# Attention by buckets, top-2 experts and a channel mix on one core: three new tables of order, engines and buffers

## The chip, the cores and the metric

The kernel runs on one core of one Trainium2 chip. The metric is the device time of one execution in microseconds (us). Before the change the median of three runs is 452.78 us (450.99 to 452.79).

## What is computed

The inputs are q, k and v of two batches, eight heads, 768 positions and 64 elements, float32. The reference has three stages, each on the result of the one before.

```python
# 1: attention inside hash buckets
q_bucket, k_bucket = buckets of the signs of q @ proj, k @ proj     # six bits each
scores = scale * q @ k.T,  -1e9 where the buckets differ
x = softmax(scores) @ v                       # heads side by side: 2 x 768 x 512
# 2: two of four experts of causal attention
w = softmax of the two largest of x @ w_gate
out = sum over e: w_e * (causal softmax(x wq_e (x wk_e).T) @ (x wv_e) @ wo_e)
# 3: channel mix, with x_prev the row before
xk = mu_k * x + (1 - mu_k) * x_prev;  xr likewise with mu_r
result = sigmoid(xr @ w_r) * (relu(xk @ w_k) ** 2 @ w_v)
```

## The kernel before

The 1536 rows of the two batches are cut into twelve row tiles of 128 (tile i belongs to batch i // 6). Each tile goes through all three stages: eight score products `s_i_h` of bucket attention, one per head, each followed by a softmax and the product with v (`x_i_g`, four heads each); the expert stage (`qk`, `vg`, scores `se`, `y`, output `o`); and the mix (`h` for the hidden layer, `r` for the gate, `v` for the way down). float32 products are made from float16 parts: an operand is split into a high part (a copy to float16) and a low part (the rest), and three products are added.

- **Softmax.** DVE takes the scores out of PSUM (`P<-s`, `P_m<-se`, with the row's extreme as its accumulated output), ACT makes the exponent in place. For twelve (tile, head) pairs, all eight heads of tile 0 and four of tile 1 (`F32T`), PE then transposes the float32 result (`tp`). For the 84 others ACT or POOL makes the high part `PHL`, POOL the low part, a transposing DMA on SP's queue turns it to `PT`, and PE multiplies `PT` with v. A product of PE on a `PT` that has not landed would wait for that DMA.
- **Mix.** DVE makes `o`, then four `m32k` and four `m32r`; `mk` and `mr` are their float16 parts. ACT makes `t` and `k2h` of the hidden layer, DVE `h` and `k2l`, and ACT the gate `e` with the sigmoid. Exp and sigmoid are functions of different tables on ACT, and the build puts an `ACT_TABLE_LOAD` wherever the next function is not in the table that is loaded.
- **Buffers.** PSUM has two slots of tag `s` for scores and four of tag `d` for everything else; SBUF has 13 large slots `b3` (P, PHL, PT, k, v), 40 `b2`, 4 `x2t` and 2 `b4`.

The program is first recorded: class `Program` takes down 2540 operations (`add`), each with its engine and the operations it must follow. Then `arrange` (line 205) applies three tables, and `issue` (line 220, whose call is L225) emits the operations in the order that the table gives. So L225 is the line of every row, and rows are told apart by engine and tile.

```python
for o, e in zip(self.ops, unpack(engines, np.uint8)):
    if e:
        o.move("PVAG"[e])
self.order = [self.ops[i] for i in unpack(table, np.uint16)]
...
for t, h in zip(tiles, unpack(homes, np.uint8)):
    if t.slot:
        t.kw.update(tag=f"{t.slot[1]}_{h}", bufs=1)
```

`ENGINES` moves a copy or a high part to DVE (V), ACT (A) or POOL (G); `Op.move` rewrites the call. `ORDER` is a permutation of the 2540 operations, and thereby the order on each engine and each queue. `HOMES` gives each tile its slot within its tag: two tiles of one slot are in it one after the other, so the later one's first writer waits for the earlier one's last reader.

Of the kernel before, what the change touches and what calls it, by code (L numbers as in the profile page):

```python
# [1001 lines left out]
C^lGHrz4@iR`LNR$l=VkgLssc-?b$1yM#HbD>g$XT!m=El2_1F~XjEQ)FH2`+>}xCkP{Jt&NMF%Q1R>9iQ~;ZdDR?O`x9!zGZLtKu7+2IJs9^n|pS4x8drOpi0@EoQ(W
kP{w2RC);0VH!oFzi<~c$FjH^_CRFX3y<J2MAL7$pM;{*K6r*F^l#h`f8d{37yrTUcmUqvbL<7<AqKt27MO=)(lPpg|Kfl61U}+Re1X^CIK`q9^b~$z2Yd!fCn-C;!jA
Y8K8F|Z5_-cax(>@RHXWe6e2@-NC(O?U_!Z>i9ki3;5YSir1vk<S_!$$@LHL3R=q7BUU38ds(@-eL@u?6O=FM~qZbK0+%JXS8Eugq`2iDLY+Cqsa3MHm^bO^T6LRv&Ks
T&sK5}XT?P<K2Gi)k&Lrge0LN^(*{oJC!*IIpK(cm$HsQd&kwAvw*aPn?4KU|&22U2!k<$8B^RdSFCYLM{0+rJ<D68++mmSWc~YIL@JgI35`X;b)#pgK-F^q6;(tS5Rj
dg@hAu626AC)S6e)2;4v;aVGS`bmXuNSL300k-qRxT%9LkTb_)m=_`-M^mJT3UZS5l19gF4SnyXqsZ($t<)Q986@O#JF*uKY=WpDDYj90|3s<No=cl}MmB!*3dIPoiJ8
!2V^bW33J}OSD=qR0~qVy;C;=i~N7oc<WE4+vE)SC-Z2`WY(AR}F;#$16vLKf=4fAC6Ik*DDe8is{v9NwgunvI%pR+@>~sU*$9+8j&U@!y<-N>NkJM9sJ(cjC@miGPDG
JOl62Et-yXcsAaqRjw=Cp$Al$N>ewOgPCbA=A^zh4_CXoyw?50^YJ{aaSJdP<)(X7ikowJT8QghX)Z%$sWO+N3RICE(tWB#OK}PI;S11}%kW}cgcl*Qt4vks5-h_(T!p
LB3am!y+(5nzQQRsl%T*a&IUd4S;3}kdzXQ3|SdYKKBdX7Xc_<&#1a25N;PO12W4eDigJbs{{(%2Dq5BioU{tpfYf^QpMK$OLH)M6uTy0WL<kn()&L-VBmNT~=H{fFmu
D*9}BW}VL{4>>|by$~@JHx)582j-NjP9P&GwRRJX#gj7v0Z&i;f~@HYDy#cFplK66vMqB@0!yneo3$B5WXgGqj?OEWpOE8GipHfs0oeZBrXX?a1H4l9mC_;g5J{!jOgO  # L1010
HllXxqa#Ebc<9P>8<~J1AZO3hx3@7k3ZbUP9CMU-!{Do5BbYAaL;#S<?GP=z;i&yeTisa(pMwi7Ub(!2$4)_br=1p$1OXjw?Ioz1m^D0i|B4B10-)(g}F(U55v@W&F>a
w})?h|cuyK%dVgsXWTf2BPb&+T)+Qd??8kueI!#os8WOXJ#5JnT-bsU0=&``r?bkDn>GJLM8!dz#O^D2Mx<deCXtftK<Cw}IF2U$6xeVo%EDI?@@}k{0k0x0W~ZPn5@X
qR!NX{)W6R5$1FETz+@Z^`@ilALvVcXou@c-{@aB=03rH(2okZg6;==r$6a0I_tX8CXTIt&|X}~QL&*1{F`>VeYhW&@c}IA{-K{BhA!fN=^*|`pWz3cbDJ4B8vYDlppg
# [86 lines left out]
```

## Time and profile before

| what | value |
|---|---|
| median of three runs | 452.78 us (450.99, 452.78, 452.79) |
| profiled execution, device time | 453.12 us |
| its span, first to last instruction | 451.3 us |
| PE busy | 430.6 us, 95% of the span |
| DVE busy | 348.4 us, 77% |
| ACT busy | 311.6 us, 69% |
| POOL busy | 347.3 us, 77% |
| PE's granted clock over the span | 1.000 |

The profile is of one execution, whose device time is 1.8 us over its span and 0.34 us over the median of the runs. A busy PE is one with a matmul in its pipeline, so its busy time is an upper bound on its work. DMA share above 1.00 in a row means that the packets of several queues overlap.

### The profile page before, as it was taken

The page shows a single profiled execution, that of the slowest core. Times are in us where ns is not written, and L with a number is a line of the kernel's source. Part 1 is how long each engine was busy: PE and PEld are TensorE (multiplying, and loading weights), DVE is VectorE, ACT ScalarE, POOL GpSimd, SP SyncE. Part 2 cuts the span into 40 slices and gives each one's busy share as a digit, 9 for nine tenths or more (in the row PEclk, how much of TensorE's full clock was granted, in tenths as well). Part 3 has the DMA queues.
Part 4 walks back from the last instruction along what each step waited for, and adds up shares of the span by engine and source line. Part 5 has one row for each costly group of instructions (what it writes and reads, how often), then busy time and mean ns, then how long its engine had stood idle before and what let it go on. Part 6 is the DMA issues. An engine that isn't in the chain of part 4 may idle for free.

```text
span 451.3 us, 14823 instructions
## 1 busy us (share of the span) xinstructions
PE 430.6 (95%) x6009; PEld 335.3 (74%) x6009; DVE 348.4 (77%) x906; ACT 311.6 (69%) x502; POOL 347.3 (77%) x375
## 2 busy tenths in 40 slices
PE   3899999989999999998999999999999999999997
PEld 2777878767888765884798668889666766976675
DVE  3799999999999998899798878766866666474432
ACT  5899979878878766787857787785456853265121
POOL 5997999998999969899999768997767856337130
...
GB/s 275 225 233 216 219 189 182 207 162 190 185 226 190 211 184 192 120 240 179 154 176 205 140 158 179 124 184 166 179 109 116 171 137 81 108 13 179 70 23 49
DMA packets 219701, 73.86 MB, mean 164 GB/s; under 512 B 211048, under 2 KB 215408, under 8 KB 219632
## 3 DMA queue, kind: packets, MB, share of 16 engines
...
## 4 chain that ended last, share of the span: by engine, by line
PE 43%; ACT 4%; DVE 4%; DMA 3%; issue 3%; POOL 3%; POOLq 0%; DVEq 0%; ACTq 0%
PE h L225 10%; PE v L225 9%; PE x L225 5%; PE s L225 4%; PE r L225 4%; DMA PT<-PHL 2%; PE qk L225 2%; PE se L225 2%; POOL PHL L225 2%; PE o L225 2%; PE vg L225 2%; PE y L225 2%; ACT P L225 2%; ACT L225 1%; DMA yT<-hl_y 1%
## 5 line engine op out<-in xcount | busy, mean ns | idle before, releaser
L225 POOL TENSOR_TENSOR PHL<-P,PHL 128x768 f16<-128x768 f32 x84 | 142.4, 1701 | 15.6 <-ACT PHL L225 13.6
L225 ACT ACTIVATE P<-P,mx 128x768 f32<-128x768 f32 x96 | 87.8, 931 | 16.2 <-DVE P L225 14.1
L225 DVE TENSOR_SCALAR_CACHE_REDUCE P<-s 128x768 f32<-128x768 f32 x96 | 90.3, 949 | 7.8 <-PE s L225 5.7
L225 PE MATMUL s<-y,x 128*128 128x384 f16 x384 | 77.5, 328 | 3.2 <-DVE P L225 3.1
L225 PE MATMUL h<-mk,WK 128*128 128x128 f16 x1152 | 74.4, 219 | 0.0
L225 PEld LDWEIGHTS <-WK 128*128 128x128 f16 x1152 | 67.7, 98 | 4.3
L225 PE MATMUL v<-WV,k2h 128*128 128x512 f16 (+1 forms) x208 | 57.8, 363 | 0.9 <-DVE y L225 0.9
L225 PEld LDWEIGHTS <-PT 128*128 128x128 f16 x1512 | 52.6, 98 | 6.2 <-issue 1.7
L225 PE MATMUL x<-vh,PT 128*128 128x65 f16 x1008 | 56.4, 194 | 0.6 <-DMA PT<-PHL 0.3
L225 PEld LDWEIGHTS <-x 128*128 128x128 f16 x480 | 38.5, 98 | 21.2 <-issue 3.5
L225 POOL TENSOR_SCALAR PHL<-P 128x768 f16<-128x768 f32 x42 | 36.7, 875 | 7.0 <-ACT P L225 5.1
L225 PE MATMUL x<-vl,PT 128*128 128x64 f16 x504 | 41.4, 193 | 0.0
L225 POOL TENSOR_TENSOR PHL_m<-P_m,PHL_m 128x512 f16<-128x512 f32 (+2 forms) x24 | 33.4, 1401 | 7.2 <-ACT PHL_m L225 6.6
L225 PE MATMUL v<-WV,k2l 128*128 128x512 f16 (+1 forms) x104 | 37.7, 363 | 0.0
L225 PE MATMUL qk<-xT,WQK 128*128 128x128 f16 x576 | 37.1, 219 | 0.0
L225 ACT ACTIVATE PHL<-P 128x768 f16<-128x768 f32 x42 | 34.9, 835 | 2.4 <-POOL PHL L225 1.5
L225 ACT ACTIVATE t<-h 128x512 f32<-128x512 f32 x24 | 14.2, 590 | 32.4 <-PE h L225 32.4
L225 PE MATMUL r<-WR,mr 128*128 128x512 f16 x144 | 35.7, 379 | 0.1
L225 PEld LDWEIGHTS <-WQK 128*128 128x128 f16 x576 | 33.7, 98 | 1.2
L225 PEld LDWEIGHTS <-k2h 128*128 128x128 f16 x208 | 18.8, 98 | 15.9 <-issue 1.5
L225 DVE SCALAR_TENSOR_TENSOR h<-h,t 128x512 f32<-128x512 f32 x24 | 16.6, 693 | 13.7 <-ACT t L225 13.5
L225 ACT ACTIVATE P_m<-P_m,bias_m 128x512 f32<-128x512 f32 (+2 forms) x24 | 19.3, 818 | 8.8 <-DVE P_m L225 8.7
(175 smaller groups left out, 928.1 us busy)
## 6 DMA issues: line engine op xcount, KB each, us to landing
...
PT<-PHL SPq DMA_TRANSPOSE x84, 4.2
```

The lines of the kernel that those rows point to most:

```text
L225: getattr(getattr(self.nc, engine), method)(*[real(a) for a in args], **{k: real(a) for k, a in kw.items()})
```

## The change

The three table strings are replaced; no other line of the kernel differs. The rows of the tables are compressed text, so the first line of each stands here for it.

```diff
 ORDER = """
-c-jTQ0{|FC3;@93Kgrj&ZQHhO+qP}nwr$(C&8;2Uxw}&kFaXF6ksuFLg}i`}56VDIr~z@I8kB_-P#p?Dfc#Jp>OeWD3-O>9)P{;s2u=Y(e24;-pfXf}!cYW~KvLKYePB
...
+c-jq@gAy3X5&(C!GaK8sZQHhO+qP}nwr$%s?~+4u&U@d`Ro&IzsWTTGJ8`*PXK)T&9v9ceb4y)bx6DOx`CNV%$yId)+;SJ+t#D;rRJYO<bP-%3*Vz?zMO-4c%2jhQTv?
...
 HOMES = """
-c-lo&*<#yB3?s<7hf1o{U2CP-a_b}i|A&ilnyeq}WJUx*0F=n*2Puj|OtOeZfkGp|3xfqg3_O;gJT~K@73mXrB;z3->G<0!qyzkqwXEXZFR`DnAFu-Z7y2&tD)L9{A9f
...
+c-l2oi+18V5Yx=~5kF|yaFgveEF>(H|Nq0QX-nWZ;Mf{TBM11tL}OOJN0<f`Q!@#iP!&ZO#6&C&FiXNg3aS_s{3E_!`2iOhZ-dA$SQZ44cah)F{{#^zzybOO{eb)d{)w
...
 ENGINES = """
-c-rk%%M!#O2$SUh|9Q95mlb4zvA3li>meW}KwEnlw*~#?Fx-Is#rKgX2x>F>b%$8X1!4P}VT>Sfat;S4eLVBCGOI)YSoP$e7(O41Zz5yDjK#taStb#vfKuQYJ<kkf<rR
...
+c-qaCQ38V?3`1$&{qMZFsVhRU;LrF#1R6>Rp_HnyRXYCk8&I)h0`;i22FDy~yicF%I5&s75?@r6bg^{jzm#5bY6)K}?B|h#WAK?;v%f`>cs^;D{oZ0Ns}9vM%Qm-lT$B
...
```

Both programs have the same 2540 operations. PE has the same matmuls (6009 in the trace of before). Some 175 operations run on another engine: of the high parts `PHL` 24 go from POOL to ACT and 19 from ACT to POOL; of the copies `y` out of PSUM seven go from ACT to DVE and four back; of the copies `x` seven from DVE to ACT and three back; and single ones of `vnh`, `x2t`, `kT`, `mr`, `mk` and others. DVE has 736 operations instead of 738, ACT 481 instead of 478, POOL 370 instead of 371. 972 of the 1279 tiles that have a slot get another one. ACT's table loads are 20 instead of 16.

The first piece is DVE's order at the beginning: `prhl` is the split of the hash projection, `nbq` and `nak` the low parts of the first query tile and of the keys. Before:

```order
L225 CAST prhl_75<-pr32_72 128x6
L225 SCALAR_TENSOR_TENSOR nbq_81<-q32_0_79,nbq_81 128x8x64
L225 SCALAR_TENSOR_TENSOR nak_0_1_1_102<-k32_0_1_1_84,nak_0_1_1_102 128x12x64
L225 TENSOR_TENSOR prhl_75<-pr32_72,prhl_75 128x6
L225 SCALAR_TENSOR_TENSOR nak_0_1_0_104<-k32_0_1_0_95,nak_0_1_0_104 128x12x64
```

And in the change:

```order
L225 CAST prhl_75<-pr32_72 128x6
L225 TENSOR_TENSOR prhl_75<-pr32_72,prhl_75 128x6
L225 SCALAR_TENSOR_TENSOR nbq_92<-q32_0_83,nbq_92 128x8x64
L225 COPY x2_0_109<-tr_x2_0_104 128x512
L225 SCALAR_TENSOR_TENSOR nak_0_0_1_96<-k32_0_0_1_94,nak_0_0_1_96 128x12x64
```

The second row of `prhl` now comes ahead of the first `nbq`, and one `nak` stands where three stood.

The second piece is DVE's order in the middle of the program. `P_6_h` takes the scores of head h of tile 6 out of PSUM, `P_m5` those of an expert of tile 5, `y_4`, `rse_4` and `y32_4` finish tile 4's experts, `vl` is a low part of v, and `qT_5`, `kT_0` are the low parts of tile 5's expert queries and keys. Before, these are rows 345 to 353 of DVE's order:

```order
L225 TENSOR_SCALAR y_4_4144<-y_4_4144,gs_4_3384 128x4
L225 RECIPROCAL y_4_4144<-y_4_4144 128x4
L225 TENSOR_TENSOR rse_4_4353<-y_4_4144,g_4_3383 128x4
L225 SCALAR_TENSOR_TENSOR vl_1_0_4202<-v32_1_0_1_4116,vh_1_0_3594 128x768
L225 TENSOR_TENSOR y32_4_4376<-y_4_4144,rse_4_4353 128x256
L225 SCALAR_TENSOR_TENSOR qT_5_4369<-qk_5_4187,qT_5_4369 128x256
L225 SCALAR_TENSOR_TENSOR nbq_81<-q32_7_615,nbq_81 128x8x64
L225 SCALAR_TENSOR_TENSOR kT_0_1248<-qk_5_4187,kT_0_1248 128x2x128
L225 TENSOR_SCALAR P_6_4_4389,mx_6_4008<-s_6_4_4342 128x768
```

In the change, rows 356 to 364, of which the last frees the PSUM slot that PE's `se_5_1_0` (second score product of tile 5's experts) is given by the new `HOMES`:

```order
L225 TENSOR_SCALAR y_4_4188<-y_4_4188,gs_4_3667 128x4
L225 RECIPROCAL y_4_4188<-y_4_4188 128x4
L225 TENSOR_TENSOR k2l_2_4152<-h_2_4_4170,k2h_2_4094 128x512
L225 TENSOR_TENSOR rse_4_4374<-y_4_4188,g_4_3666 128x4
L225 TENSOR_SCALAR P_6_6_4404,mx_6_3928<-s_6_6_4378 128x768
L225 TENSOR_TENSOR y32_4_4406<-y_4_4188,rse_4_4374 128x256
L225 TENSOR_TENSOR z_q7_4362<-z_q7_4362,zl_q7_4402 128x8x6
L225 TENSOR_SCALAR nbq_92<-z_q7_4362 128x8x6
L225 TENSOR_SCALAR P_6_4_4411,mx_6_3928<-s_6_4_4355 128x768
```

`h_2_4` and `k2l_2` of the mix and the evictions `P_6_5`, `P_6_6` now stand around the same `y_4` chain, and `kT_0` of tile 5 has gone further ahead.

The third piece is ACT's order around the first sigmoids: `e_0<-r_0` and `e_1<-r_1` are sigmoids, `P_5_h` in place the exponent of head h of tile 5, `WV2` and `wd_v2` the weight split. Before, directly after one `ACT_TABLE_LOAD`:

```order
L225 ACTIVATE e_1_3082<-r_1_2997 128x512
L225 ACTIVATE PHL_m3_1_3115<-P_m3_1_2861 128x512
L225 ACTIVATE wd_v20_0_3134<-raw_v20_0_3043 128x512
L225 ACTIVATE e_0_3141<-r_0_3096 128x512
L225 ACTIVATE yT_2_3152<-tr_y_2_3146 128x256
L225 ACTIVATE WV2_0_3169<-wd_v20_0_3134 128x512
L225 ACTIVATE wd_v25_0_3190<-raw_v25_0_3102 128x512
L225 ACTIVATE PHL_5_2_3226<-P_5_2_3025 128x768
L225 ACTIVATE x2t_2_2204<-o_2_3209 128x4x128
L225 ACTIVATE WV2_5_3260<-wd_v25_0_3190 128x512
L225 ACTIVATE vnh_0_524<-vg_4_3245 128x4x64
L225 ACT_TABLE_LOAD
```

In the change:

```order
L225 ACTIVATE WV2_5_3238<-wd_v25_0_3178 128x512
L225 ACT_TABLE_LOAD
L225 ACTIVATE e_0_3240<-r_0_3162 128x512
L225 ACTIVATE wd_v20_0_3306<-raw_v20_0_3153 128x512
L225 ACT_TABLE_LOAD
L225 ACTIVATE P_5_6_3244<-P_5_6_3244,mx_5_2902 128x768
L225 ACTIVATE WV2_0_3337<-wd_v20_0_3306 128x512
L225 ACT_TABLE_LOAD
L225 ACTIVATE e_1_3339<-r_1_3302 128x512
L225 ACT_TABLE_LOAD
L225 ACTIVATE P_5_4_3277<-P_5_4_3277,mx_5_2902 128x768
```

Two sigmoids that stood under one load now have a load each, with an exponent between them.

## Rows read from the trace of the kernel before

**Rows 1.** The page's part 1: PE's busy us, share of the span, instructions.

```profile
PE 430.6 (95%) x6009; PEld 335.3 (74%) x6009; DVE 348.4 (77%) x906; ACT 311.6 (69%) x502; POOL 347.3 (77%) x375
```

**Rows 2.** PE's waits: waiting row, releaser, us in total, times, longest us.

```profile
PE tr_x L225 <- DVE nbq L225: 6.6, 1, 6.6
PE s L225 <- DVE P L225: 3.1, 4, 1.0
...
PE tr_x L225 <- DVE kT L225: 0.6, 1, 0.6
...
PE x L225 <- DMA PT<-PHL: 0.3, 1, 0.3
```

**Rows 3.** The page's part 6: KB each is left out, us to landing.

```profile
PT<-PHL SPq DMA_TRANSPOSE x84, 4.2
```

**Rows 4.** Windows of the span, busy us of each engine (instructions), overlapping stretches.

```profile
core 0: us, PE busy (x) PEld busy (x) DVE busy (x) ACT busy (x) POOL busy (x), PEclk, DMA share, GB/s
0.00:30.00 30.00, 20.68 (x230) 16.73 (x230) 20.08 (x49) 22.12 (x39) 22.91 (x39) 1.00 0.91 255
...
60.00:90.00 30.00, 28.38 (x468) 23.75 (x466) 29.02 (x78) 25.78 (x47) 28.92 (x31) 1.00 1.08 202
...
0.00:122.00 122.00, 107.48 (x1376) 89.48 (x1377) 108.40 (x265) 103.24 (x188) 106.81 (x133) 1.00 0.95 210
0.00:152.20 152.20, 137.68 (x1857) 113.88 (x1858) 136.73 (x343) 128.14 (x232) 136.22 (x165) 1.00 0.98 210
0.00:211.83 211.83, 194.77 (x2683) 157.61 (x2684) 190.18 (x465) 173.10 (x296) 189.94 (x217) 1.00 0.99 201
211.83:451.34 239.51, 235.88 (x3326) 177.64 (x3325) 158.23 (x442) 138.51 (x207) 157.36 (x159) 1.00 0.75 130
```

**Rows 5.** Timelines of DVE and PE: start us, us, row [idle before <-releaser].

```profile
211.37 0.41 DVE L225 SCALAR_TENSOR_TENSOR kT<-qk,kT 128x256 f16<-128x256 f32 x1
...
211.83 0.38 PE L225 MATMUL tr_x<-ident,nbq 128*128 128x128 f16 x4 [0.60 <-DVE kT L225]
```

**Rows 6.** The chain of waits, 205 to 226: start us, us, what, count.

```profile
218.25 0.67 PE v L225 x3
218.92 1.30 PE se L225 x14
220.22 0.45 PE tr_x L225 x8
...
220.89 1.10 PE x L225 x36
```

**Rows 7.** DVE by form: busy us, mean ns of one, idle before it, releasers.

```profile
L225 DVE TENSOR_SCALAR_CACHE_REDUCE P<-s 128x768 f32<-128x768 f32 x96 | 90.3, 949 | 7.8 <-PE s L225 5.7 <-POOL PHL L225 0.8 <-PE x L225 0.6
...
L225 DVE SCALAR_TENSOR_TENSOR m32r<-o,mu,x2t 128x128 f32<-128x128 f32 x48 | 15.6, 342 | 0.2
...
L225 DVE DVE_READ_ACCUMULATOR P<-s 128x1 f32 x96 | 7.8, 82 | 0.0
...
L225 DVE SCALAR_TENSOR_TENSOR WK<-wd_k,WK 128x512 f16<-128x512 f32 x8 | 5.5, 682 | 0.0
...
L225 DVE SCALAR_TENSOR_TENSOR kT<-qk,kT 128x256 f16<-128x256 f32 x12 | 5.0, 416 | 0.2
...
L225 DVE COPY x<-tr_x 128x512 f16<-128x512 f16 x11 | 4.5, 415 | 0.2 <-ACT x L225 0.2
L225 DVE COPY y<-tr_y 128x768 f16<-128x768 f16 x8 | 4.4, 554 | 2.2 <-PE tr_y L225 2.2
```

**Rows 8.** ACT by form, the table loads.

```profile
L225 ACT ACT_TABLE_LOAD x16 | 20.5, 1283 | 3.9 <-issue 2.0 <-PE r L225 1.4 <-DVE P_m_p L225 0.2
```

**Rows 9.** Timeline of DVE at the start.

```profile
5.70 0.17 DVE L225 CAST prhl<-pr 128x6 f16<-128x6 f32 x1 [5.70 <-DMA pr<-in_proj_dram]
...
7.92 0.15 DVE L225 TENSOR_TENSOR prhl<-pr,prhl 128x6 f16<-128x6 f32 x1
```

More of the change, by code (lines that the diff above doesn't have):

```diff
@@ L1002 @@
[L1002 to L1013, printed above, removed]
@@ new lines @@
+46`&NPb5XG&RD{w{1J<~)F00Gt=DBfhryK9OyWuVut#zp&hbsfMAsWtil^~~^<QhXXZ3J~72Q-0oZZy_}o~{<Ogw(LWMaOX%17l(u7=!sCC#-i1-FV#K#^NH^7TUXv&>
+AYkQ7r(OV1mm9?Vt)Qb`fx+TjDmkHqg<vf?n>p7KGleJpiVMLXa6Ix{p*CcDc0B%d)@-R|GP^UH2>GhKRV^MZ%G;C?Ixnc_AJ2alb)U$On0Va0T~uv2X%@f~Jt&?QxOu
+o;#*{-9&5#lQ0`hcE7_uHwBx+Wc&<eAv@f658P{b1N&W7_z9l4srb+xaEyXe+*B7+pTIPH3U%QvJaUg+3pk<E@h|urW}wIVGRu91XYdPrgHi4n9(2cXntSGchCg6Geu3
+QdCp>lkKoool{oHqW?q0a(kjtIGjTjqW!6uA@C$R&(bl2P~_X0L!Z~GS#;eYS}w%`vqg$FRQ>j-)1BW%U~E&*P516(KAfv52uEXDV5!|lYln3wWVLcHl#<1XBdd+;FMa
@@ new lines @@
+`|Z)DjvcDblWY*_&D1Yq?wo)4`U%JOi6H#yW<>g!)|ciCB;K-79Mu<u{+Gh6}TK$ViB6|y1)@vluFQ17Y}E+u5iq)!M#|Fj=MQH7kj~4>;b)@4-}`K&>xava=d^?Z~+d
+7g_r^_;s{uWqu>)Q!q3zf)?+NKMkQ%9T*7{E85iS77!Q*GU=<F8K`;PP;{>QqUECF%4D)azq{1{f7&77%nCr&CRlJ5%Aw3R(p-_XyLI%u&DUl!>B4o!**pkxXPqYEQP)
+*8=>97^$!LO7Tvtn!dna*H7%z^olVHh06C0GOna$+qifWOeMR1~{YF1+BzL2;bv3gQeXgdTd(G$?`7L7^C4bdBgY+K!EBAAX}*(1vEhY&eT^peLQfOD;EdpxRUt=fXVr
+ok~$D>_zjT3ALs3cpWdhj#QeixCO8fuDYhwn_jy&?gkddoA}n%p-%Lj{-i&s8I_?j_!m{6cdj!nh0<6a+fg4{49#f?l*2`^3@Xxl*VT1%3Aiqm#TBp~KDdu=6Wqm>0Nj
@@ new lines @@
+O;%hDiP$@S<qmZPq;8dgCCyn`FzS2u(zVkP{W5<?}bOjT$g)u)6^Tp6q2KXeQKr3bhH?qOA`imP}qt%341l<HsudWh99Ij?2rweTMeBjLWLd>>cyZ!QI|;p%Ao2!GIUY
+Dnw&clXT&{_dXQAFd`w=0qHUYhewH!tLoX{^{01On#0pur|KLsBG{IV{uAO0^KMbdv+X=ThLKB1W)i4zQ(>(7Y{=NjKuw@KSkrDFn~r-G8jq8Aq5<PQIrzu<6EqUO>r`
+fr7?62HbZQV&g1Af#NiXr44Y#rPRvPo8a2U&n3_+*2b@7M_#GzW_521KVGEo>6Dd7!;L)^^H}iP<8RK(Wo=LN46F0^QG@B;TREh%`cnfdi>6C>7Y~_qRhq7`{i~zr2ck
+F@N`Bz*?UoaxX<xJc_vT-E%h>_tdzQ;72ls{oF{0*bPJc<jeXgzI#c)Sf(Q)cdsx%e-ao##_Si3fdfA8&`Pu!MHNXIx70Ap!Koez=Bmat_|X3uq_&j{A8R<mNn_m)Fuy
@@ new lines @@
+xQtriH*AX==oIgUgpdf@;6hqQ8|eTqr@!4I%Ex;kKWFp*xB|SBcX2`f16$)ke#+l*F8%9@@+SHd|HA*=Za&0CxG<mQLcD_h#(yv>9N~ZQKio`v_{abA+YZ~~8Ggn;&`}
+Bg<j(Rrj-k<@CGLfzyqNaEekjR6(V+t#;|_8Fig9ti$3z#nBgTO9yp^`obB+nI;2<35`+S1;GLzD07aN4O(M3MVFL(=G=NsG!e{v7FGj_q3T$O)zUtCxG>bl`2M!L+0c
+?b2BowSQ~(`)|4^~Y=ckY~vNJgJ_HqR}JnD6jYm55%3)M4HMVyvb2%Fb0ZF5hx-J!A=s1Vo)zRLQi-oHj>72m;2cpe#^b36c599d<weCa4gHG;TGTKGcZ7AOJsV?-DHj
+olz!4#HpniCLT90m^q20^Lz>AsI1i<{HecnKRE<A!bE(edc(=5WzH*1la|N!*mAI9Z;VyCkE<!A7?Dt4z{=_ZifDDpLuunEh9X=?7r3TmJO;UyT${yNFLu4N{;QcZ}hR
@@ new lines @@
+J*0F2iN0)a7QpRdz@{-X`Pa18<ShvRTH+1ZgeJ`H<X}&-@b~mY=!5wULH=N2W`CZox<7xU}S2JXU5%#&A?l$T4XvD`k~@;n+G?&PqEOCvoU2pO;^_i61GAxG^{33$j>N
+%RGrohiHwgmHBc`MoDa1APZ%t+?6HrM&eO?Iw_~*8!wgLI03cdU%4s&&J*Rd9Hgc`AuW>wl!%tgTR9_t@^{`(hiQ_eq(1fs|HYH#owVjDlA4avF*;9Y=?tBt<K(3cuag
+%3y_}%+($YtgRCJP3P#TIXQ>DGM<z`;xo_vt|(%h$|cASnL$RfEYQKXe`&mA~Db>tQDRBp&LIi-JdYyV6-aa3vJ+xkoLP@c;tc_KIE6y1_`{<4_7mc;ZQN0%4!NSwrw>
++*v^P(I5QY41Nu66)xq$xreRC#4SlUyds;<^Qsj$C8XX`5;#%g2a@e{*`q087L$DDw*h-bn(e4vHUE<d~}T^vE?*Hl%Bpf5BDSdSIJCSC@aO2Y_z~<r}(nacl8P67s){
@@ new lines @@
+n>5IgX5!lPe(V1T4H~C%S>Nkm}@in0&&<FHg`ukZviFEV5{YXE+&-R@;q5dJG{e9}ff65sDh$i__zPs<?lS(4#;|Kb_zAOJLlYMu-K;1ZzKBhr_tY74x&|u%sr_iS~$M
+@v9KA9w!6p~U>NosjUJ@~Yq(SIb34DtWT-!joJ^A{<lp4DDF!}sBF{+y2Yefhj*k|}<k&lJ+>Rr(>9s2|Vw;1lZrp5O;FdgoK=V&9*K@l>B)r}^oAxz8X&xV%=-6+VMr
+rYw3vlW0aA%29l3y+XI>Hr=6gvc#|S*JzcG>SOqddY#tz8<a`Y=uL{|SNp7bm*V=RKBiAAX*IK^m%k*s&!*3*gx;fAKDLkN<NKtVQ4;zDKAFCtm$cSr*MVF~6Zw*wLo-
+WapTt+zbv~D5ll8uo=9Vn7!IOVQ*(IxZub%yDDyVNLkC=Z;mm#^v@ufAF=9P`UkZ$rxz4+W(MuU&wBl<`_vM;XXG>_)hca%>z`<$9X?rP>xK$H1<dQmUweck3?>U&D=K
@@ new lines @@
+j=ptV3)P94zv{hffmt}e!EZQQ~R8f#t*Wpy463{qB_`yST(J#RkXa6lP$i6ruFIkD}Al${T0m;cKGX>!I#ziT0w5;L%pfBwXE#)U-cI)rcbnv?($c)roPdkR#7tgTDsf
+U)yh&yp6WBLB3VN{t*@DVCjUtP&@BE}&FU}sK|G2_@-5BoZ|i6t!`HNc-{Z&fIKJrL>T|uL`Fwsqou_dQ|3a_$OFp-s!8v^{|4H}yKlLvi&jtN&+CVqkXWj2-av^`&f7
+j!Fi(U2C{C~R7PvGD6z0Tq<`c2>IL4U#@@+bY@`jeja2Yf>vX2b0tU1Mu)osF;`|6j(!a@ZG?pLGrwl6f}C3dnUon~(UTK96V1>l^96I^Rax8Na|5+EPP1_5Wa;^+jYZ
+7n7p?m@n*a_~L%D74u+4WxW;gCHy)6f4rt<7A%4-v#nOjkFhCM*^ja+zM?PbEBVHnEi}>dzNt3Th_=D1`r=aBSNBux12xy%zM5~Ti|mfyX3MRNui<a`R=UDwSPQ-B@A|
@@ new lines @@
+SnduXjQZI<=djaJUjwrMunR@y4N=eJvVU%}t^IYQ2mJLC%ObT~io19Yqn)Q3K*MY1UN$UpWwteZaZ&-`HRu221Q|HAjsURu-F@;$YU*7oD9gVynN{YxLiUipstlb>TFc
+)Z25$QI4&`Su#!+G>6O(I>S7_Qp5xL$sk!X1z6|<p~q4lkT^C(plg7PkxYg(a%1Uz4NhbuI;qx_S#S6#nwmr>O{+7$!!u(=Ajzf(pXOGs%dSQ#<h6%vw!b1TNazbOKd9
+dv#hqs@=M;Z+VX{YyvugmUfW~yc>$LU2knsc(-byb4_m2_&FX{?{;U7Rmk+=C-+W5TAL@o9Hc~5uqn64>XdGL}zx&ae-9~BE@ZB%sZ~hPe!ymK4p<YO5@hyQRv_zKJDh
+AN>RyyP|r@1YUrM4tCM#pM_u$WKSI32G`xLPP+U;G4}p%Zl}|K~GUek&4=8|oyj6i825J}VPih3a7$vx?@mf>y{1TM;W5T8C*`Kb*FrVX{^ZXRJYJ9HwZEFjfEjzcf?}
@@ new lines @@
+g|eYan65LmNoW&lhLdKxP@9GYTGY<kT>Z<Rvs?DJFBZ<*KYorb(#1MkZ`&-rU=2gt&>@ty;-OrarzJwryY{cI9qw2JZ5J-tBdZlkNVCv9Jhv9%rQNgk;k~sCC8d-!3Z*
+5YM$*XIF+8?Tp_mo7&Y^3#Z)K!QcwtfWl~t81cGbFtYBFCxSocs}dW4>#S14g0?TKBq(pJ)zY46Y{^bMtKrGBz&cHLgv61{9SWQEq0<+@7C*c*Fb53QEemO667%2~fq-
+OAe<tzdPfq74W&teW)?Rc&CXWW&OsFgOeeTXblc7@pc{eQT3KO?zga?W?`B$>ArP8S2Setz}cfR-GD_>d*GYMuyShrft?SVQiQcezDy;JM7V4?Kc}2_UiC3BK&UK^qXz
+hQQ^Do)Olf@?$ZUKvMmc$Y)+UKriVXly>8GQx>4tcUAkWn=<={4%m^z(Ya1V0+CTP}Ee!wJCaq(C+TXS)%nhw<aaa-#>V&W~w6MBX+y1p5R?i^#fI))`AyBYT-#9d|h8
@@ L1057 @@
+ZA{Pwpp_xVT#;K+9z!TJcijZC1uMBK8J00EYW{=7M_L|Vax%g
 """
```

57 lines of the change are left out of this document (16 added, 41 removed).

## Prediction

> **What bounds the kernel now.** I read the page's first part, then PE's waits, then the span in windows, and last single rows. The first part says that PE is the engine of this kernel: 95% of the span [rows 1]. Its waits say how little of the rest is due to late transposes. The only row with a `PT` as releaser is one wait of 0.3 us, and the largest is the start, 6.6 us until DVE has made the first `nbq` [rows 2], although a transposing DMA takes 4.2 us from issue to landing [rows 3]. With that 0.3 and a few shorter stalls of under 0.1 to 0.45 us in the timeline, I put all that PE loses to late landings at no more than 1.1 us (an estimate). A table that leaves three times the room for such landings can therefore win about a microsecond by that alone.
>
> The windows show where PE's time goes instead. In the first 211.83 us PE is busy 194.77, so it stands still for 17.1; in the other 239.51 it is idle for 3.6 [rows 4]. In the first stretch DVE is busy 190.18, POOL 189.94 and ACT 173.10. PE's own work is less than its busy time: its rows take 0.67 us per three `v`, 1.30 per fourteen `se`, 1.10 per 36 `x` when they follow one another [rows 6], and by such intervals it has 180 us of work ahead of the row at 211.83. That row is a transpose of the query tile 7, released by DVE's `kT` of 211.37 after 0.60 us of idle [rows 5]. From there on DVE has far less to do than PE, 158.23 us in 239.51 [rows 4]. So up to this point PE can run no faster than DVE frees PSUM for it, with POOL hardly behind; after it PE sets its own pace. **The time is DVE's first 212 us plus PE's last 239.5.**
>
> DVE's 212 us are 190.2 of work and 21.65 of idle. The idle is uneven: 9.92 in the first 30 us, 3.68 between 30 and 122 (4.0%), 8.05 between 122 and 211.83 [rows 4]. Of the first 9.92, 5.70 is the wait for the hash projection [rows 9].
>
> **The change part by part.**
>
> *The middle of DVE's order.* In the changed order the row with the same 180 us of PE's work ahead of it is the first product of `se_5_1_0`, whose slot is freed by the eviction `P_6_4`. PE's rows ahead of it differ: 54 `x`, 14 `se`, 8 `tr_x` and 8 `z_q` more, 9 `r` and 6 `v` fewer. By the intervals of [rows 6] that is 1.65 + 1.30 + 0.45 + about 0.2, less 15 rows at 0.22, thus 3.35, so within 0.3 us of nothing. DVE's rows ahead of it differ by more. By the order, one eviction of `P` and two of `P_m` are done earlier: 3 x (0.949 + 0.082) = 3.1 us [rows 7]. By the engine table, three copies `y` more (1.66), three copies `x` fewer (-1.25), one high part each of `WK` and `WR` more (1.36), one `x2t` more (0.69, taken like `WK`, a row of the same size), four 128x256 copies of which two come and two go (0), and one copy of `PF` less (-0.55, taken like `y`): 1.9. Small rows make 0.2. So DVE must have done 190.2 + 5.2 = 195.4 us of work before PE can go on, instead of 190.2.
>
> What this costs depends on DVE's idle, which the trace of before can't show for the new order. The ends are the best stretch that it has, 0.98 us of 30 between 60 and 90 (3.3%) [rows 4], and all the idle that it has now, 21.65. I take the rate of 30 to 122, since there DVE is the bound without interruption, which with 5.2 us more of work in front is what the new order asks of it for the whole stretch. Then t = 195.4 + 9.92 + 0.040 x (t - 30), t = 212.6: **0.8 us later**. At 3.3% it is 211.2 (-0.6), with the old idle 217.0 (+5.2).
>
> *The start.* `prhl`'s second row, 0.15 us [rows 9], stands ahead of the first `nbq`, behind the landing at 5.70. PE's first matmul comes 0.15 later; but DVE does that row in either order, so it is in the sum of DVE's work already: 0. That three `nak` make room for other rows, and k lands in another sequence, could close some of the 4.2 us that are idle beside the landing, or open more; I keep 9.92 and give half of it, 2.1, to the good end.
>
> *The copies moved between ACT and POOL.* 24 `PHL` go one way and 19 the other; in the first 152.2 us ACT is idle for 24.1, POOL for 16.0, over 211.83 us 38.7 and 21.9 [rows 4]. Five high parts of under a microsecond are hidden there: 0. Without that cover they would be 4 us.
>
> *Four table loads more.* 4 x 1.283 = 5.1 us on ACT [rows 8]. The first extra pair stands around the first sigmoids, in the stretch in which ACT has those 24 us; the second falls after 211.83, where ACT is busy 138.51 of 239.51 [rows 4]. I cost them at 0; the other end is 5.1.
>
> *The new slots.* 972 tiles change places, which shifts who waits for whom; what that gives or takes is in the rate of DVE's idle above, and not a term of its own.
>
> *The last stretch.* PE's work there is the same, so 239.5 stays. At the very end the gate of tile 11 is moved up: its `r` can start 5.4 us earlier, right behind `h`, and then rests on a chain of `o`, eight `m32` at 0.342 [rows 7] and `mr` on two engines, some 7.2 us where PE has 7.1 us of other work: 0.3 at most, charged. Waits for late landings: at best -1.1, taken as 0, since the room, counted through both orders by PE's intervals between the last product that a transposed tile depends on and its first use, is not larger where it is smallest: 4.7 us before and 4.4 now (median 11.2 and 12.2).
>
> The sum against the profiled run: 453.12 + 0.8 + 0.3 = 454.2. The median of the runs is 0.34 lower, so **453.9 us**.
>
> **The rivals.**
>
> *Slower: DVE keeps its idle.* Its waits at the handovers with PE, ACT and POOL stay at 21.65 us, since they come from the chain score, eviction, exponent, split, which the tables don't shorten. Then the extra 5.2 us lie in front of PE's point in full: 452.8 + 5.2 + 0.3 = 458.3. It is slower by over 0.5% from an idle of about 18.3 us on (17.2 of the forecast and the 1.1 from 453.9 to 455.0). For it: DVE's idle between 122 and 211.83 is 9% and not 4% [rows 4]. Against it: part of that idle is time in which DVE waits for PE itself (the `PE s` among the releasers of `P` [rows 7]), and that vanishes when DVE lies further behind.
>
> *Faster: a denser DVE.* With the longer rooms fewer rows of DVE and PE stand behind a late one. DVE runs at 3.3% idle, and the start gives 2.1 us: 211.2 - 2.1 - 211.83 = -2.7 us, the late waits give another 1.1: 449.0 us. For it: between 60 and 90 us DVE did run so, with nearly the same mixture of rows. Against it: the start is bound by landings and by rows that the change does not shorten.
>
> *The change doesn't do what it says.* Late landings cost a microsecond at most, the smallest room is not larger, and the orders are equally good by luck: 452.8, no difference.
>
> *Table loads on the path.* In the new order of ACT the exponent `P_5_4` stands behind two sigmoids and four loads, `P_5_6` behind one sigmoid and two loads. If the rows around them are just in time, as ACT's own waits before a load (3.9 us for all 16 [rows 8]) hint, up to 5.1 us come on top: 459. Against it stand 24 us of idle on ACT. [...]
>
> **How the numbers follow.** A difference of 0.5% (2.3 us: under 450.5, over 455.0) is about what a measurement of this kernel can tell from none. The forecast has 0.45; with the rate of idle between 3.3% and 5% it spans 452.5 to 456.2, and I count 0.36 of it as no difference and 0.09 as slower. The slower rival with the old idle has 0.20, the table loads 0.03, both slower. The faster rival has 0.22. No effect has 0.10, the same. That makes faster 0.22, same 0.46, slower 0.32. The range runs from the faster rival to the slower one, 449.3 to 458.2, and leaves the outer half of each, about 2 in 10, outside.
>
> **What would show it.** Right: PE's waits still have hardly a `PT` in them; DVE's busy time up to the first `se_5_1` is 195 us, its idle 17, and that row starts between 212 and 213.5; the rest of PE's work takes 239 to 240 us; ACT has 20 loads, and no wait of PE's of over 0.5 us ends at a sigmoid or at the exponent behind one. The forecast is wrong if that row starts below 210 or above 216, which the two rivals say, or if PE's last stretch changes by more than 2 us, which none says: then PE's own work or its waits behind the DVE-bound stretch were misjudged.

## The result and the profile after

The changed kernel takes 454.81 us (median of seven runs, 452.85 to 455.56), the kernel before 452.09 us in the seven runs that go with it (449.58 to 452.79). The ratio is 1.0062, with a 95% interval of 1.0037 to 1.0087: 2.7 us slower, just over the 0.5% that the prediction set as the bound. The forecast was 453.9; of its three cases "no difference" had 0.46 and "slower", which it was, 0.32.

The two profiled executions alone would say the opposite. The changed kernel's was the shortest of its seven (452.85 us, span 451.0), while that of before, 453.12 us, lies above every one of its seven runs. So the readings below use more than one profile of each list of DVE's work.

The page's first part, to be read beside [rows 1], has PE at the same share; DVE's and POOL's busy times are 346.2 and 346.0 us, ACT's is 317.5 (four table loads make 5.1 of its 5.9 us more):

```profile
PE 427.9 (95%) x6009; PEld 333.0 (74%) x6009; DVE 346.2 (77%) x904; ACT 317.5 (70%) x509; POOL 346.0 (77%) x374
```

PE's waits after the change (columns as in [rows 2]):

```profile
PE tr_x L225 <- DVE nbq L225: 6.5, 1, 6.5
PE tr_x L225 <- DVE x L225: 1.6, 2, 1.1
PE qk L225 <- DVE kT L225: 1.4, 1, 1.4
PE tp L225 <- DVE WR L225: 1.4, 1, 1.4
...
PE s L225 <- DVE P L225: 0.8, 1, 0.8
```

No row of this view names a `PT` any more; before, one did, with 0.3 us. The waits for `P` went from 3.1 to 0.8, and new waits of over a microsecond for DVE's `kT`, `WR` and `x` stand in their place. DVE still releases PE, and none of its waits of over 0.5 us ends at a sigmoid or at an exponent.

The windows, cut at 212.70 us, where PE begins `se_5_1`, the row that the prediction named (columns as in [rows 4]):

```profile
0.00:30.00 30.00, 19.07 (x232) 15.42 (x233) 22.07 (x51) 22.49 (x40) 21.52 (x40) 1.00 0.93 263
30.00:122.00 92.00, 85.61 (x1149) 72.38 (x1147) 88.22 (x219) 81.15 (x151) 86.41 (x91) 1.00 1.02 198
122.00:212.70 90.70, 88.29 (x1376) 69.26 (x1375) 82.97 (x207) 72.58 (x114) 82.41 (x84) 1.00 0.98 187
0.00:212.70 212.70, 192.97 (x2753) 157.06 (x2754) 193.26 (x475) 176.23 (x302) 190.34 (x213) 1.00 0.99 202
212.70:451.00 238.30, 234.93 (x3258) 175.96 (x3257) 152.91 (x430) 141.23 (x208) 155.63 (x161) 1.00 0.76 129
```

Against [rows 4], DVE has done 193.26 us of work at PE's point instead of 190.18 and been idle for 19.4 instead of 21.65. The stretch behind the point takes 238.3 instead of 239.5. The timelines of DVE and PE at that point, which answer to [rows 5]: the eviction `P_6_4` that frees the slot, then PE's last wait before the row that has the slot next, and that row.

```profile
211.37 0.95 DVE L225 TENSOR_SCALAR_CACHE_REDUCE P<-s 128x768 f32<-128x768 f32 x1
```

```profile
206.31 0.82 PE L225 MATMUL s<-y,x 128*128 128x384 f16 x4 [0.34 <-DVE P_m L225]
...
212.70 1.15 PE L225 MATMUL se<-kT,qT 64*128 64x384 f16 x12
```

Unlike the row of [rows 5], this one did not have to wait: its slot was free at 212.3 us, and PE had worked without a pause since 206.31, where DVE last held it up. The point is thus a mark of equal work of PE, 6.4 us behind the last wait for DVE.

### The profile page after: what moved, and what is told of

It reads as the page before. It is cut to its first block, busy times and chain, and to the rows that moved or that the text cites. A ratio compares the mean times of both kernels' runs of the same rounds, so it can differ in the third digit from the quotient of the medians.

```text
span 451.0 us, 14800 instructions
## 1 busy us (share of the span) xinstructions
PE 427.9 (95%) x6009; PEld 333.0 (74%) x6009; DVE 346.2 (77%) x904; ACT 317.5 (70%) x509; POOL 346.0 (77%) x374
## 4 chain that ended last, share of the span: by engine, by line
PE 53%; POOL 3%; DVE 3%; issue 2%; ACT 2%; POOLq 0%; DVEq 0%
PE v L225 12%; PE h L225 9%; PE r L225 6%; PE x L225 6%; PE s L225 6%; PE qk L225 3%; PE o L225 2%; PE se L225 2%; PE y L225 2%; PE vg L225 2%; POOL PHL L225 2%; PE tr_y L225 1%; DVE P L225 1%; ACT P L225 1%; DVE hl_x L225 0%
## 5 line engine op out<-in xcount | busy, mean ns | idle before, releaser
L225 POOL TENSOR_TENSOR PHL<-P,PHL 128x768 f16<-128x768 f32 x84 | 142.5, 1705 | 23.2 <-ACT PHL L225 20.6
L225 DVE TENSOR_SCALAR_CACHE_REDUCE P<-s 128x768 f32<-128x768 f32 x96 | 90.4, 950 | 19.4 <-PE s L225 13.3
L225 ACT ACTIVATE P<-P,mx 128x768 f32<-128x768 f32 x96 | 88.4, 934 | 19.0 <-DVE P L225 16.2
L225 PE MATMUL s<-y,x 128*128 128x384 f16 x384 | 76.8, 326 | 1.2 <-DVE P L225 0.8
L225 PE MATMUL h<-mk,WK 128*128 128x128 f16 x1152 | 74.4, 219 | 0.1
L225 PEld LDWEIGHTS <-WK 128*128 128x128 f16 x1152 | 68.2, 98 | 7.0 <-issue 0.4
L225 PEld LDWEIGHTS <-PT 128*128 128x128 f16 x1512 | 53.2, 98 | 6.8 <-issue 1.5
L225 PE MATMUL v<-WV,k2h 128*128 128x512 f16 (+1 forms) x208 | 57.6, 362 | 0.2 <-DVE WV L225 0.2
L225 PE MATMUL x<-vh,PT 128*128 128x65 f16 x1008 | 56.7, 193 | 0.0
L225 PEld LDWEIGHTS <-x 128*128 128x128 f16 x480 | 37.5, 98 | 19.4 <-issue 1.5
L225 ACT ACTIVATE t<-h 128x512 f32<-128x512 f32 x24 | 14.2, 590 | 42.1 <-PE h L225 42.1
L225 PE MATMUL x<-vl,PT 128*128 128x64 f16 x504 | 41.4, 193 | 0.0
L225 ACT ACTIVATE PHL<-P 128x768 f16<-128x768 f32 x47 | 39.1, 837 | 2.9 <-POOL PHL_m L225 2.2
L225 PE MATMUL qk<-xT,WQK 128*128 128x128 f16 x576 | 36.4, 219 | 1.6 <-DVE kT L225 1.4
L225 PE MATMUL v<-WV,k2l 128*128 128x512 f16 (+1 forms) x104 | 37.7, 363 | 0.0
L225 POOL TENSOR_TENSOR PHL_m<-P_m,PHL_m 128x512 f16<-128x512 f32 (+2 forms) x24 | 35.2, 1468 | 1.4 <-ACT PHL_m L225 0.5
L225 PE MATMUL r<-WR,mr 128*128 128x512 f16 x144 | 35.8, 379 | 0.1
L225 PEld LDWEIGHTS <-WQK 128*128 128x128 f16 x576 | 33.5, 98 | 3.2 <-issue 1.9
L225 POOL TENSOR_SCALAR PHL<-P 128x768 f16<-128x768 f32 x37 | 31.9, 867 | 4.5 <-PE x L225 1.7
L225 DVE SCALAR_TENSOR_TENSOR h<-h,t 128x512 f32<-128x512 f32 x24 | 16.6, 692 | 17.6 <-ACT t L225 17.6
L225 PEld LDWEIGHTS <-k2h 128*128 128x128 f16 x208 | 18.4, 98 | 11.6 <-issue 0.2
```

The costliest lines, as they stand in the source:

```text
L225: getattr(getattr(self.nc, engine), method)(*[real(a) for a in args], **{k: real(a) for k, a in kw.items()})
```

## The experiments

Two theories stood against each other first. A is the prediction's: DVE's list up to PE's point got longer, and the rest is as before. B is one that the runs themselves brought up: most runs of the change have a mean granted clock of 0.992 to 0.996 and the profiled one 1.000, so a lower clock of PE might cost the time. The count of operations that move to another engine is 155 (the text on the change has some 175).

A fence marked as a diff gives an edit in short. Where tables are exchanged or spliced, the kernel that ran has other strings in them, and names such as `ENGINES_OF_THE_OTHER` stand for these. L228 and L229 are the call of L225 below inserted lines.

**The change again.** No edit.

> The change itself once more, for more runs and a second profile. Theory A (the stretch that DVE bounds got 0.8 us longer, the rest is as before): again 454 to 455 us, 0.4 to 0.7% over the kernel before; in the profile se_5_1 of the first batch starts at 212 to 214.5 us, the rest takes 238.5 to 240 us. Theory B (the granted clock of PE falls below 1.00 for a while in most executions of the changed kernel, and not in the profiled one of 452.85 us): runs with a mean clock of 1.000 lie at 453 and below, those at 0.992 to 0.996 between 454.3 and 455.6, and a profile of such a run has a window with PEclk under 1.00 in which PE's rows take longer, while DVE's work up to se_5_1 is 193 us as in the first profile.

Measured: 456.37 us (454.60 to 457.50), ratio 1.0097 (1.0065 to 1.0129). The profile is of the run with 454.60 us. Its windows (columns as in [rows 4]):

```profile
0.00:214.43 214.43, 194.46 (x2753) 158.98 (x2754) 193.28 (x475) 176.41 (x302) 190.64 (x213) 0.99 0.98 201
214.43:452.70 238.27, 234.93 (x3258) 175.92 (x3257) 152.91 (x430) 141.27 (x208) 155.88 (x161) 1.00 0.76 129
```

The time is higher than theory A had it. DVE's work up to the point and the length of the last stretch are the same as in the first profile to 0.03 us; all that differs is 1.7 us of DVE's idle. They are there in full at 61 us already. PE's rows in the first profile of the change, then here, and a window from here:

```profile
19.91 0.83 PE L225 MATMUL tr_y<-ident,nbk 128*128 128x128 f16 x12 [0.78 <-DVE nbk L225]
61.08 0.55 PE L225 MATMUL tp<-ident,P 128*128 128x128 f32 x3 [1.36 <-DVE WR L225]
```

```profile
20.80 1.44 PE L225 MATMUL tr_y<-ident,nbk 128*128 128x128 f16 x12 [0.78 <-DVE nbk L225]
62.79 0.55 PE L225 MATMUL tp<-ident,P 128*128 128x128 f32 x3 [1.38 <-DVE WR L225]
```

```profile
20.00:25.00 5.00, 4.16 (x44) 3.71 (x44) 4.34 (x17) 4.16 (x7) 4.64 (x10) 0.66 0.89 244
```

Some 0.9 us are there at the first of these rows: PE's first row of all already started that much later (7.42 us instead of 6.49). The other 0.8 come behind it, in a stretch in which PE's granted clock read 0.50 from 21 to 24 us (for about 3.4 us by the mean of 0.66 in the window above) and twelve transposes took 1.44 us instead of 0.83. That is the window that theory B expected in such a profile. Runs with a mean clock of 0.989 also lie highest here (456.98 to 457.50).

**More work for DVE in the kernel before.** Ten rows on a tile that nothing else uses.

```diff
         for n, o in enumerate(self.order):
+            if n in (511, 571, 653, 709, 770, 827, 896, 968, 1029, 1087):
+                self.nc.vector.scalar_tensor_tensor(j, j, 0.5, j, op0=OP.mult, op1=OP.add)
```

> The kernel before, with ten rows more on DVE (128x256, some 0.5 us each, on a tile that nothing else uses, so the output is unchanged), spread between 65 and 195 us. It measures the step of the prediction that decided: what 5 us more DVE work ahead of PE's point cost. Theory A (DVE's idle falls as DVE lies further behind): 0.8 to 2 us over the kernel before, DVE's idle up to its kT of 211 falls from 21.6 to 17 or 18. The slower rival (idle stays): 5 us more, 457. If DVE is not what bounds PE there: no difference.

Measured: 456.91 us, ratio 1.0099 (1.0071 to 1.0127), 4.7 us more. DVE's rows by form and the windows:

```profile
L227 DVE SCALAR_TENSOR_TENSOR junk<-junk 128x256 f32<-128x256 f32 x10 | 9.0, 900 | 0.0
```

```profile
0.00:216.11 216.11, 196.36 (x2683) 157.83 (x2684) 198.75 (x476) 173.94 (x296) 190.74 (x217) 1.00 0.96 197
216.11:455.20 239.09, 235.66 (x3326) 177.57 (x3325) 157.04 (x442) 138.50 (x207) 157.77 (x159) 1.00 0.74 130
```

A row took 0.9 us and not 0.5, so DVE got 8.6 us more to do ahead of `kT`. Its idle fell from 21.65 to 17.4, and PE's point came 4.3 us later than in the profile of before, half of the work added (6.3 us later than in the two other profiles of that list, below). DVE does bound this stretch, and the last one has hardly changed (239.1). The idle is what theory A expected, the time nearly what the slower rival did, as the rows were longer than planned. The prediction's own formula gives 216.1 us for 198.75 us of work, which is what was measured. These ten rows wait for nothing and nothing waits for them.

**The two engine tables exchanged.** Order and slots of one kernel with the engines of the other.

```diff
-nc.arrange(ORDER, HOMES, ENGINES)
+nc.arrange(ORDER, HOMES, ENGINES_OF_THE_OTHER)
```

> The order and the slots of before, with the engines of the change alone (16 table loads, since the order is the old one). Theory A: of DVE's 5.2 us only the 1.9 us of moved copies come, and they fall into DVE's idle: 452.1 to 453.5. If the engine table is the harmful part by itself: 454 and more. If it is a gain that the order spoils: under 451.

> The order and the slots of the change, with the engines of before. Theory A: DVE has 3.3 instead of 5.2 us more ahead of se_5_1 (the three evictions stay): 453.5 to 454.5, that is 0 to 1 under the change. If the order is good and the engines harm: 452 or less. If order and engines only fit each other: above 456, with waits of PE for ACT, DVE or POOL of over 1 us that the change does not have.

Measured: 494.25 us for the old order with the new engines (ratio 1.0928, 1.0895 to 1.0962) and 494.79 for the new order with the old engines (1.0943, 1.0912 to 1.0975). Only the cases without an upper end are met, 454 and more for the first and above 456 for the second (order and engines only fit each other); a cost of some 40 us was not expected. The old order's waits of PE with the new engines:

```profile
PE tr_x L225 <- DVE nbq L225: 8.7, 4, 6.5
PE h L225 <- POOL mk L225: 4.3, 3, 3.5
PE r L225 <- DVE k2l L225: 3.5, 1, 3.5
```

So neither table is good or bad by itself, and "the moved copies cost 1.9 us on DVE" can't be tested by moving them back: the order was drawn up around them. The slots went with the order in both runs, so `HOMES` was not tried by itself.

**Warmed kernels.** Sixteen products of zeros on PE in the 6.5 us in which it waits for the first landing.

```diff
+        self.nc.vector.memset(j[:, 0], 0.0)
+        for n in range(16):
+            self.nc.tensor.matmul(w[:, 0, :], j[:, 0, :128], j[:, 0], start=True, stop=True)
```

> The kernel before, with sixteen products of zeros (128x512, no use of the result) on PE ahead of its first transposes, in the time in which it waits for the first landing. In the profile of before six transposes take 0.62 us up to 20 us and 0.33 us after it. Theory B (PE's lower level at the start costs): six transposes take 0.33 us from the first on, and the time falls by 1 to 2 us. Theory A (DVE bounds PE up to 212 us): the transposes get shorter, and the time changes by less than 0.7 us.

> The same sixteen products in front of the changed kernel. Theory B: no window with a granted clock under 1.00 any more, and 2 to 4 us under the 456.4 of the second look at the change, so that it lies within 1.5 us of the warmed kernel before. Theory A: within 1 us of 456.4, and still 3 to 4 us over the warmed kernel before, since what is longer is DVE's list.

Measured: 451.33 us for before (ratio 0.9985, 0.9966 to 1.0003) and 455.65 for the change (1.0077, 1.0052 to 1.0102). Eight transposes in the warmed kernel before, ahead of the same row without the products (timelines of PE):

```profile
6.78 0.61 PE L229 MATMUL tr_x<-ident,nbq 128*128 128x128 f16 x8
```

```profile
6.56 1.04 PE L225 MATMUL tr_x<-ident,nbq 128*128 128x128 f16 x8 [6.56 <-DVE nbq L225]
```

The first rows do get shorter. Later the granted clock falls to 0.50 in both, after a stretch in which PE was busy for 2.99 of 5.40 us and 1.64 of 5.50, here in the windows of the kernel before and of the change:

```profile
7.00:12.40 5.40, 2.99 (x47) 2.31 (x45) 4.42 (x10) 5.26 (x9) 3.88 (x7) 1.00 1.10 344
12.40:19.20 6.80, 5.90 (x80) 5.48 (x81) 5.59 (x13) 5.57 (x10) 6.36 (x10) 0.50 0.97 250
```

```profile
7.00:12.50 5.50, 1.64 (x29) 1.26 (x26) 4.09 (x6) 2.73 (x6) 3.01 (x6) 1.00 1.07 335
12.50:15.90 3.40, 3.09 (x28) 2.83 (x29) 2.90 (x6) 2.53 (x4) 3.17 (x4) 0.50 0.89 275
```

The warmed kernel before is 0.7 us faster by the ratio (1.3 by the medians), between the two expectations, and the change, within 1 us of its second set of runs, stays 4.3 us over it. The windows up to PE's point and behind it, the kernel before first:

```profile
0.00:209.85 209.85, 197.84 (x2699) 157.83 (x2700) 188.91 (x466) 172.61 (x296) 189.19 (x217) 0.98 1.03 203
209.85:449.40 239.55, 235.86 (x3326) 177.57 (x3325) 157.28 (x442) 138.84 (x207) 157.79 (x159) 1.00 0.75 130
```

```profile
0.00:213.94 213.94, 197.43 (x2770) 158.12 (x2770) 193.73 (x476) 176.27 (x302) 191.28 (x213) 0.99 0.99 201
213.94:452.20 238.26, 234.93 (x3258) 175.91 (x3257) 152.90 (x430) 141.27 (x208) 155.84 (x161) 1.00 0.77 129
```

The kernel before has the lower mean clock of the two up to PE's point (0.98) and the shorter span, and DVE's idle in the first 30 us is nearly the same in both (8.9 and 8.6 us). So the clock is not the cause of this difference.

**Late landings made on purpose.** A load of 256 KB that nothing uses, ahead of every second transposing DMA of the first 205 us, 25 in all.

```diff
         for n, o in enumerate(self.order):
+            if n in SECOND_TRANSPOSES:
+                self.nc.sync.dma_start(j32, q[0, :, 0:P, :].rearrange("h s d -> s h d"))
```

> The kernel before, with a load of 256 KB that nothing uses ahead of every second transposing DMA of the first 205 us on SP's queue (25 loads), so that transposes land later by a microsecond or more. If room for late landings matters: PE's waits for PT<-PHL grow from 0.3 to over 5 us and the time by 5 us or more. If the smallest room of 4.7 us (by PE's order) is enough: under 2 us more, with PE's waits for PT under 1 us.

> The same 25 loads in the changed kernel. If the change holds its promise (three times the room): it loses at least 3 us less by the loads than the kernel before does, and no wait of PE for PT. If it does not (smallest room 4.4 against 4.7, median 12.2 against 11.2): it loses as much as the kernel before, within 2 us.

Measured: 471.21 us for before (ratio 1.0404, 1.0365 to 1.0443), 18.6 more than without the loads, and 469.24 for the change (1.0372 over the kernel before, 1.0349 to 1.0394), 13.6 more than the warmed change on the same chip. PE's waits, the kernel before first:

```profile
PE s L228 <- DVE P L228: 7.8, 5, 3.3
PE x L228 <- DMA PT<-PHL: 6.7, 9, 2.1
...
PE y L228 <- DMA PT_m_p<-PHL_m_p: 1.8, 2, 1.4
```

```profile
PE x L228 <- DMA PT<-PHL: 8.7, 7, 2.3
...
PE y L228 <- DMA PT_m_p<-PHL_m_p: 1.8, 2, 1.3
...
PE s L228 <- DVE P L228: 0.8, 1, 0.8
```

The change loses some 5 us less, so it bears these loads better. It is not by fewer waits for `PT`, which are somewhat longer (10.5 us in the rows shown, 8.5 in the kernel before), against what was expected. The loads cost it less elsewhere: the wait for `P`, in which DVE had fallen behind, stays at 0.8. (DVE, ACT and POOL stand idle longer as well, DVE in the kernel before for 41.3 us ahead of PE's point instead of 21.65; the runs don't part that from the transposes.)

**Halves of both.** Up to an operation in the order and with the engines of one kernel, the rest as in the other; a tile keeps its slot where that is free, otherwise it takes the one longest free (110 of 1267 tiles in the first of the three).

```diff
+first = ORDER_ONE[:1418]
+order = first + [o for o in ORDER_OTHER if o not in first]
+engines = [ENGINES_ONE[o] if o in first else ENGINES_OTHER[o] for o in range(2540)]
```

> The first 1418 operations of the old order (up to some 225 us) with the old engines, then the rest in the new order with the new engines; slots kept where they are free, 110 of 1267 tiles moved. Theory A' (the change loses in the stretch up to the 180-us point of PE, 2 to 3 us, and wins 1.2 us behind it, 239.5 to 238.3): 1.2 us under the kernel before, 450.5 to 452, with a last stretch of 238 to 238.8 us behind the old point. If the loss lies behind the point, or the whole order only works as one: 455 and more.

> The other way round: the first 1418 operations of the new order with the new engines, then the rest as before. Theory A': the slowest of the pair, 1 to 1.5 us over the change, 456.5 to 458. If the loss lies behind the point: as before, 451 to 453.

> Only the first 426 operations (up to some 72 us) in the old order with the old engines, the rest new. Theory A' (the loss of about 2 us gathers between 60 and 212 us, where DVE has 3 us more to do): within 1 us of the change, 455 to 456.5. Theory C (it is the start: another sequence of landings and a sparser PE, and the spells at the lower granted clock there): as before or under it, 450.5 to 453.5.

For these, theory A' had the profiles so far in it: the loss ahead of the point, a gain of 1.2 us behind. Theory C puts the loss at the start. Measured: 460.92 (ratio 1.0193, 1.0168 to 1.0219), 475.47 (1.0519, 1.0490 to 1.0549) and 464.43 us (1.0288, 1.0259 to 1.0316; here the cut is at 426). All three miss: every seam opens waits of its own, as this one at 426, in PE's waits:

```profile
PE s L225 <- DVE P L225: 6.0, 2, 5.7
PE y L225 <- DMA PT_m_p<-PHL_m_p: 2.4, 1, 2.4
```

What lies clear of a seam can still be read. Windows of the old half with the new rest, of the new half with the old rest, and of the last stretch of the new kernel behind the old start:

```profile
0.00:209.80 209.80, 193.79 (x2684) 157.38 (x2685) 189.54 (x465) 173.04 (x296) 189.09 (x217) 1.00 1.00 203
```

```profile
0.00:214.29 214.29, 194.56 (x2753) 158.82 (x2754) 193.35 (x475) 176.32 (x302) 190.51 (x213) 0.99 0.99 201
```

```profile
223.76:462.00 238.24, 234.91 (x3258) 175.88 (x3257) 152.82 (x430) 141.25 (x208) 155.67 (x161) 1.00 0.73 129
```

The old half reaches PE's point at 209.8, the new one at 214.3, and the new last stretch takes 238.2, even with its start 11 us later. Theory A' holds in these pieces; theory C was not settled, since the seam at 426 covers what the start may give.

**Two table loads less.** In the change the exponent `P_5_6` goes behind the sigmoid `e_1`.

```diff
-LOAD, e_0, wd_v20, LOAD, P_5_6, WV2_0, LOAD, e_1, LOAD, P_5_4
+LOAD, e_0, wd_v20, WV2_0, e_1, LOAD, P_5_6, P_5_4
```

> The change with one row of ACT moved: the exponent P_5_6 goes behind the sigmoid e_1, so two of the twenty table loads fall away. The rival of the table loads (5.1 us on the path): 2.6 us under the change, 452.5 to 454. Theory A' (ACT has 24 us of idle there): no difference from the change beyond 1 us.

Measured: 456.06 us, ratio 1.0092 (1.0070 to 1.0114), where the change itself had 1.0062 and 1.0097. ACT by form:

```profile
L225 ACT ACT_TABLE_LOAD x18 | 23.1, 1283 | 2.2 <-issue 1.9
```

```profile
0.00:216.50 216.50, 195.17 (x2752) 159.60 (x2752) 192.60 (x475) 173.83 (x300) 191.12 (x213) 0.98 0.98 199
```

Two loads less gain nothing. The edit is not clean, though: in its profile the moved exponent starts 3.8 us later than in the second profile of the change, 0.7 of which PE was late before, and PE has waits of 0.48, 0.19 and 0.46 us between 171 and 176 us that it doesn't have there, which could hide a small gain. That the loads are hidden is seen better in the first profile of the change: the four loads around the first sigmoids stand between 156.2 and 164.7 us, and PE is busy for 53.29 of the 53.60 us from 121.0 to 174.6. At the 1.283 us that the runs show for a load, two loads on the path would be 2.6 us (an estimate); the run shows no gain.

## Why the prediction came out as it did

Profiles with either list of DVE's work, from the windows up to PE's point and behind it (us). Left out are the runs with the added loads and the one with a seam ahead of the point.

| kernel | PE's point | DVE's work ahead | DVE's idle ahead | of it behind 30 us | behind the point |
|---|---|---|---|---|---|
| before | 211.83 | 190.18 | 21.65 | 11.7 | 239.5 |
| before, warmed | 209.85 | 188.91 | 20.9 | 12.1 | 239.6 |
| old half, new rest | 209.80 | 189.54 | 20.3 | 11.4 | (seam) |
| change | 212.70 | 193.26 | 19.4 | 11.5 | 238.3 |
| change again | 214.43 | 193.28 | 21.2 | 11.6 | 238.3 |
| change, warmed | 213.94 | 193.73 | 20.2 | 11.6 | 238.3 |
| new half, old rest | 214.29 | 193.35 | 20.9 | 11.6 | (seam) |
| change, two loads less | 216.50 | 192.60 | 23.9 | 13.2 | 238.3 |
| before, ten rows more on DVE | 216.11 | 198.75 | 17.4 | 8.5 | 239.1 |

- **What bounds the kernel: right.** The time is DVE's stretch up to PE's point plus a last stretch that PE sets. The second is the same to 0.12 us (238.24 to 238.36) in six profiles of the change and its variants, whatever their start does, and the added work on DVE shows in the first alone. POOL is the rival that no run parts from DVE: it is as busy ahead of the point, and by the means of the seven profiles that have one or the other list its work there grew by 1.3 us (189.4 to 190.7).
- **Late landings: right.** With waits for `PT` of 0.3 us in all there was nothing to win, though the rival "it doesn't do what it says" is wrong too: with landings made late, the change loses about 5 us less.
- **The sum of DVE's extra work: the counted rows are right, the rest of the list got shorter.** 5.2 us were counted; the mean of the four profiles of the new list (without the one with two loads less, whose edit changes this stretch) is 193.4, of the three at the old 189.5, so 3.9. The rows that were counted are there with the lengths that were counted. But rows that both lists have took less, most of all the seven low parts `vl`, here from DVE's rows by form up to the point, before and in the change:

```profile
L225 DVE SCALAR_TENSOR_TENSOR vl<-v,vh 128x768 f16<-128x768 f32 x7 | 11.7, 1673 | 0.1
```

```profile
L225 DVE SCALAR_TENSOR_TENSOR vl<-v,vh 128x768 f16<-128x768 f32 x7 | 10.3, 1486 | 1.3 <-POOL vh L225 1.3
```

- **DVE's idle: the step that failed.** "I take the rate of 30 to 122" put the 4% of that stretch on everything up to the point. That makes 7.3 us of idle behind the first 30 us and 17.2 in all, and prices the extra work at 0.8 us. Measured are 11.5 to 11.6 behind the first 30 us in all four profiles of the new list, about as much as in the old one (11.4 to 12.1). The windows of the first profile say where: 30 to 122 does keep its 4% (3.78 us), but 122 to the point has 7.73 us (8.5%), as it had 8.05 (9%) before. The slower rival named that 9%, and had it right that the waits stay. Over the whole stretch the mean idle of these profiles fell only from 20.9 to 20.4, so nearly all of the extra work arrives at PE's point: 213.8 against 210.5, 3.3 us later, of which 0.3 lies between the eviction and PE's row. With ten rows that wait for nothing the idle did shrink, to 8.5 us behind the first 30; whether their freedom is the reason is not shown.
- **The last stretch: not forecast.** It was left at 239.5 with 0.3 us charged for the end, and takes 238.3. PE's idle there fell by only 0.26 us (3.63 to 3.37). Its busy time fell by 0.95, with 68 rows fewer, so most of the 1.2 us seems to be work that the new order does ahead of the point (the prediction's count by intervals had 0.3), and it is then in the 3.3 us as well.
- **The total.** 3.3 - 1.2 = 2.1 us by these profiles. The medians say more: 2.7 in the first comparison, 4.2 in the second set of runs and 4.3 in the warmed pair. The three profiled executions of the change are the shortest of their runs, 1.5 to 2.0 us under the medians. The forecast of +1.1 reached 453.9 with two errors that partly cancel, 2.5 us too little at the point and 1.5 too much behind it; that it came within 1 us of the result is in part luck. It was also built on an execution of before that was late by some 2 us at the point; the other two profiles of the old list reach it at 209.8.
- **The clock: a share, not the cause.** All runs on record of the two kernels that list a clock can be compared at the same mean clock: at 0.999 to 1.000 the change takes 453.9 us (2 runs) and the kernel before 452.0 (24); at 0.995 to 0.996 454.7 (6) and 452.1 (6); at 0.992 455.4 (3) and 453.1 (9). Some 2 us of the loss are thus there at each of these clocks. Below 0.992 there are only runs of the change, at 457.0 to 457.5, and they raise its median.
- **Table loads and copies between ACT and POOL at nothing:** for the loads it is shown by PE's work beside them, with 0.31 us of idle in 53.60; the copies couldn't be tested alone.
- **The signs that it named.** The row began at 212.7 us in the first profile, within 212 to 213.5, and at 213.9 to 214.4 in the next three profiles, outside it but short of 216 (216.5 only with a row of ACT moved). DVE's work was 193 us instead of 195, its idle 19.4 to 21.2 instead of 17, the last stretch 238.3 instead of 239 to 240. ACT has 20 loads, as forecast.

What stays open is what makes PE's first row and the spells at the lower clock differ between runs of the change, which spread from 452.9 to 457.5 us, and what POOL and the new slots have in the loss.
